# Two attention pairs per AV burst with the last keys as array quarters, and two transposes moved to the first mean, in a fused attention and FFN kernel

## The chip, the cores and the metric

The kernel runs on one core of one Trainium2 chip. The experiments ran in three groups, each on another chip (the record numbers them 6, 14 and 15), and every ratio is taken against the kernel before in the same group. The metric is the device time of one execution in microseconds (us). A profile of one execution belongs to each kernel; its span is about 2 us shorter than the time of a run. PE is TensorE (matmuls), PEld its weight loads, DVE VectorE, ACT ScalarE, POOL GpSimd, SP the queue that issues most of the small DMAs.

## The reference

```python
def _attn_ref(q, k, v):                       # 8 batches, 12 heads, 448 tokens, 64 dims
    scores = (1 / sqrt(64)) * q @ k.T
    attn = np.maximum(scores, 0.0) ** 2 / 448
    return attn @ v

def _moe_ref(x, g_ln, w_ch1, w_ch2):          # x: (8, 448, 768), the heads side by side
    xn = (x - mean(x)) / sqrt(var(x) + 1e-6) * g_ln
    return x + np.maximum(xn @ w_ch1, 0.0) @ w_ch2        # 768 -> 3072 -> 768
```

There is no softmax: relu squared keeps every score independent, so scores, squares and AV can be cut into pieces at will.

## The kernel before

For each batch b the kernel runs a first FFN layer (24 columns of 128 hidden units, `ffn_1`), then a second one. While it runs the first layer of batch b, it does the attention of batch b+1 in short "excursions" between two columns. A "pair" is two heads; a batch has six. Scores of a pair come in slots of 128 keys (t = 0, 1, 2); the last 64 keys (t = NF = 3) of two pairs share one slot, as four 64x64 quarters of the PE array. A batch has 21 slots of scores (QK), three in each of seven excursions, E1 to E7 below.

AV of one pair takes four slots: three of 128 keys, and one for the last 64 keys, whose weights `v_rest` are padded with zeros to 128 rows. One excursion does at most one AV:

```python
def att_AV(i, half=None, bank=None, evac_by=None):
    b, pr = divmod(i, NPAIR)
    if half != 1:
        av[0] = (next_f() if bank is None else bank)[:, :S]
    ps = av[0]
    v_heads, v_rest = v_parts(b)
    order = [NF, 0, 1, 2] if i % 2 else [0, 1, 2, NF]
    for n, t in enumerate(order):
        if half is not None and n // 2 != half:
            continue
        for hh in range(2):
            if t < NF:
                weights, values = v_heads[:, 2 * pr + hh, t * D:(t + 1) * D], attn[i, t][:, hh, :]
            else:
                weights, values = v_rest[:, pr, row0(i, hh):row0(i, hh) + D], attn[i - i % 2, NF][:, i % 2, :]
            nc.tensor.matmul(ps[hh * D:(hh + 1) * D, :], weights, values,
                             start=(n == 0), stop=(n == NF))
    if half == 0:
        return
    if evac_by is nc.scalar:
        nc.scalar.mul(xT_of(b, pr), ps, c2)
    else:
        nc.vector.tensor_scalar(xT_of(b, pr), ps, c2, None, op0=Alu.mult)
# ... (loads of the next v, sums for the mean)

def ffn_1(ni):
    ps = next_f()[:, :S]
    for ki in range(K1):
        for c in range(2):
            n0 = ni * P + c * D
            nc.tensor.matmul(ps[c * D:(c + 1) * D, :], w1[:, ki, n0:n0 + D], xc[:, ki, :],
                             start=(ki == 0), stop=(ki == K1 - 1))
    nc.scalar.activation(h[:, ni, CARRY:], ps, Act.Relu)

def excursion(n, third=(nc.vector, nc.vector), **how):
    flush_loads()
    next_AV(**how)
    took = [slots.pop(0) for _ in range(n)]
    for m, (i, t) in enumerate(took):
        att_QK(i, t, relu_by=third if m == 2 else nc.scalar)
    for i, t in took:
        att_square(i, t)
    for i, t in took:
        for e in ends(i, t):
            ready.append(e)
            queued(e)
```

The kernel uses eight banks of PSUM, the memory that the matmuls write to. Four (`sc`) hold scores, two (`spare`) hold the third QK slot of an excursion, and two (`next_f`, in turn) hold FFN columns and AV results. So a column uses bank A, the AV bank B, the next column A again: nobody waits for a bank.

Batch 0 has nothing to hide behind, so its attention comes first, slot by slot. Its end, where the mean over the features has to be known before the FFN can start, is this:

```python
def first_end():
    i = NPAIR
    att_AV(i - 1, 0)
    att_QK(i, 0)
    att_QK(i, 1)
    mean_part(i - 2)
    att_AV(i - 1, 1)
    mean_part(i - 1)
```

Batches 0 and 1 are transposed on PE (`att_T`), later ones by DMA transposes on the SP queue.

Of the kernel before, what the change touches and what calls it, by code (L numbers as in the profile page):

```python
# [11 lines left out]
def kernel(  # L12
# [44 lines left out]
    t_pool = ctx.enter_context(tc.tile_pool(name="qkT", bufs=3))  # L57
    attn_pool = ctx.enter_context(tc.tile_pool(name="attn", bufs=7))
    st_pool = ctx.enter_context(tc.tile_pool(name="stats", bufs=4))
    acc_pool = ctx.enter_context(tc.tile_pool(name="acc", bufs=4))  # L60
    o_pool = ctx.enter_context(tc.tile_pool(name="o", bufs=3))
    ps_pool = ctx.enter_context(tc.tile_pool(name="ps", bufs=1, space=bass.MemoryType.PSUM))
# [53 lines left out]

    next_sc = Turns(sc).next
    f_turn = Turns(fb[:2])
# [130 lines left out]

    def att_T(i, copy=None):  # L250
        if i >= PE_T * NPAIR:
            new_qkT(i)
            nc.sync.dma_start_transpose(qkT[i], qk_ring[:, i % 3].rearrange("p j c -> p (j c)"))
            return
        new_qkT(i)
        if i == 0:
            for t, cp in enumerate((nc.vector.tensor_copy, nc.scalar.copy)):
                ps = bf_view(next_f())
                pe_T(0, t, ps)
                c = slice(t * S, (t + 1) * S)  # L260
                cp(flat(0)[:, c], ps[:, c])
            return
        ps = bf_view(next_f() if i <= NPAIR else next_spare())
        for t in range(2):
            pe_T(i, t, ps)
        (copy or nc.vector.tensor_copy)(flat(i)[:, :2 * S], ps)
# [34 lines left out]
    def xT_of(b, ki):  # L301
        return xT[:, ki, (b % 2) * S:(b % 2 + 1) * S]

    def att_AV(i, half=None, bank=None, evac_by=None):
        b, pr = divmod(i, NPAIR)
        if half != 1:
            av[0] = (next_f() if bank is None else bank)[:, :S]
        ps = av[0]
        v_heads, v_rest = v_parts(b)
        order = [NF, 0, 1, 2] if i % 2 else [0, 1, 2, NF]  # L310
        for n, t in enumerate(order):
            if half is not None and n // 2 != half:
                continue
            for hh in range(2):
                if t < NF:
                    weights, values = v_heads[:, 2 * pr + hh, t * D:(t + 1) * D], attn[i, t][:, hh, :]
                else:
                    weights, values = v_rest[:, pr, row0(i, hh):row0(i, hh) + D], attn[i - i % 2, NF][:, i % 2, :]
                nc.tensor.matmul(ps[hh * D:(hh + 1) * D, :], weights, values,  # L319
                                 start=(n == 0), stop=(n == NF))  # L320
        if half == 0:
            return
        if evac_by is nc.scalar:
            nc.scalar.mul(xT_of(b, pr), ps, c2)
        else:
            nc.vector.tensor_scalar(xT_of(b, pr), ps, c2, None, op0=Alu.mult)  # L326
        if i >= PE_T * NPAIR and i % 2 and i + NPAIR < NP_ALL:
            load_v(i - 1 + NPAIR)
        if b == 0:
            if pr < GAIN_FIRST:  # L330
                nc.vector.tensor_scalar(xc[:, pr, :], xT_of(b, pr), g_sb[:, pr:pr + 1], None, op0=Alu.mult)
        elif pr == 1:
            nc.vector.tensor_add(xs, xT_of(b, 0), xT_of(b, 1))
        elif 1 < pr < NPAIR - 1:
            nc.vector.tensor_add(xs, xs, xT_of(b, pr))
# [55 lines left out]

    def ffn_1(ni):
        ps = next_f()[:, :S]
        for ki in range(K1):
            for c in range(2):
                n0 = ni * P + c * D
                nc.tensor.matmul(ps[c * D:(c + 1) * D, :], w1[:, ki, n0:n0 + D], xc[:, ki, :],  # L397
                                 start=(ki == 0), stop=(ki == K1 - 1))
        nc.scalar.activation(h[:, ni, CARRY:], ps, Act.Relu)  # L399

# [9 lines left out]
    def new_o():  # L410
        o_t = o_pool.tile([P, HD], fp32, tag="o")
        return o_t

    def store(o_t, m, d0, d1, engines=(nc.sync,)):
# [18 lines left out]
    def plain_part(b, m, dh, part, parts, box):  # L433
# [10 lines left out]
        if part == parts - 1:  # L444
            o_t = acc_pool.tile([P, HD], fp32, tag="acc")
            scaled_plus(o_t, box[m], m, x_half(m, dh))
            store(o_t, m, dh * HD, (dh + 1) * HD)
# [22 lines left out]
    def seven(b, pair, banks, last, between):  # L470
# [5 lines left out]
        bb = c  # L476
        acc1 = acc_pool.tile([P, HD], fp32, tag="acc")
        acc2 = acc_pool.tile([P, HD], fp32, tag="acc")
        tt = nc.vector.tensor_tensor
# [65 lines left out]
        if last:  # L545
            cut = HD - P
            parts = ((bb, 0, cut), (spare[1], cut, HD))
            for ps, d0, d1 in parts:
                product(ps, sums[6], B_TOP, True, d0, d1)
                flush()  # L550

                def after(ps=ps, d0=d0, d1=d1):
                    o_t = new_o()[:, :d1 - d0]
                    scaled_plus(o_t, ps[:, :d1 - d0], m2, acc2[:, d0:d1])
                    store(o_t, m2, HD + d0, HD + d1, (nc.sync, nc.scalar))
                posts.append(after)
            flush()
# [20 lines left out]
    for i in range(NPAIR, NP_ALL, 2):  # L578
        first = [(i, t) for t in range(NF + 1)]
        if i % NPAIR == 2:  # L580
            first[2:] = first[:1:-1]
        slots += first + [(i + 1, t) for t in range(NF)]
    slots = slots[slots.index((NPAIR, 2)):]
    ready = []

    def ends(i, t):

        if i % 2 == 0:
            return [i] if t == (NF - 1 if i % NPAIR == 2 else NF) else []
        return [i] if t == NF - 1 else []  # L590
# [5 lines left out]
    def excursion(n, third=(nc.vector, nc.vector), **how):  # L596
        flush_loads()
        next_AV(**how)
        took = [slots.pop(0) for _ in range(n)]
# [9 lines left out]
    def step_fine(i):  # L609
# [29 lines left out]
        if i:  # L639
            mean_part(i - 1)  # L640
        att_AV(i, 1)
        att_square(i + 1, 2)

    def first_end():
        i = NPAIR
        att_AV(i - 1, 0)
        att_QK(i, 0)
        att_QK(i, 1)
        mean_part(i - 2)
        att_AV(i - 1, 1)  # L650
        mean_part(i - 1)

    def ffn_1_first():
# [19 lines left out]
    IN_FIRST = (5, 8, 11, 14, 17, 20)  # L673
    T_IN_FIRST = {4: 1, 7: 2, 10: 3, 13: 4, 16: 5}
    X_AT = (4, 6, 8, 10, 12, 14)
# [4 lines left out]
    def ffn_1_all(b):  # L680
        ms = tiles_of(b)
        for ni in range(NI0 if b == 0 else 0, K2):
# [4 lines left out]
            if b == 0 and ni in V_AT:  # L687
                load_v(V_AT[ni])
            ffn_1(ni)
            flush()  # L690
# [12 lines left out]
            elif b < B - 1:  # L703
                shift = 2 if b == 1 else 0
                if ni - shift in IN_REST:
                    excursion(3, **(dict(third=(nc.scalar, nc.vector), evac_by=nc.scalar) if b == 1 else {}))
                if ni == min(IN_REST[-1] + shift + 3, K2 - 1):
                    flush_loads()
# [70 lines left out]
    with tc.manual_schedule(engines=set(ENGINES)):  # L779
        load_heads(0, [("q", 2, 2), ("k", 2, 2), ("k last", 2, H - 2), ("q", 4, 4), ("k", 4, 4), ("v", 0, 4),  # L780
                       ("v last", 0, H), ("q", 8, 4), ("k", 8, 4), ("v", 4, 4), ("v", 8, 4)])
        load_early()
        load_heads(1, [("q", 0, 2), ("k", 0, 2), ("k last", 0, H)])
        load_w1(0)
        load_heads(1, [("q", 2, 4), ("k", 2, 4)])
        load_w1(1)
        load_w1(2)
        load_heads(1, [("v", 0, H), ("v last", 0, H), ("q", 6, 6), ("k", 6, 6)])
        for c in range(3, NCH):
# [54 lines left out]
```

## Time and profile before

| | before |
|---|---|
| time, median (4 runs) | 528.01 us (527.81 to 528.66) |
| span of the profile | 525.9 us |
| PE busy | 517.0 us, 98% |
| granted PE clock | 1.0 |
| first-layer stage, batches 2 to 6, each | 37.72 us |

The page of the kernel before, part 1 (busy time of each engine, share of the span, instructions), and two of its costliest groups (line, engine, operation, tiles, shapes, count, then busy us and mean ns of one, then idle time of the engine just before them and what ended most of it):

```profile
PE 517.0 (98%) x5705; PEld 309.9 (59%) x5705; DVE 375.3 (71%) x662; ACT 272.8 (52%) x444; POOL 221.8 (42%) x255
...
L397 PE MATMUL f<-xc,w 128*64 128x448 bf16 x2256 | 226.9, 354 | 0.7 <-DVE o_t L428 0.4
...
L319 PE MATMUL f<-at,v_ring 128*64 128x448 bf16 x336 | 40.3, 354 | 0.5 <-DVE xT L326 0.2
```

PE has practically no idle time, and the first layer (L397) and AV (L319) are two of its largest pieces. But "mean 354 ns" is not what a matmul costs here: matmuls overlap, and two column halves run together. What one costs is read from start to start. The timeline of the kernel before around excursion E4 of one batch, PE only (start us, length us, engine, line, operation, tiles, shapes, count):

```profile
166.13 3.60 PE L397 MATMUL f<-xc,w 128*64 128x448 bf16 x36
169.56 0.92 PE L319 MATMUL f<-at,v_ring 128*64 128x448 bf16 x8
170.41 0.38 PE L279 MATMUL sc<-qkT_t 64*64 64x448 bf16 x4
170.72 0.36 PE L284 MATMUL sc<-qkT_t 64*128 64x448 bf16 x2
170.92 0.35 PE L284 MATMUL f<-qkT_t 64*128 64x448 bf16 x2
171.21 0.57 PE L397 MATMUL f<-xc,w 128*64 128x448 bf16 x4
```

From 166.13 to 169.56 there are 36 matmuls, 18 concurrent pairs: 0.19 us for one slot of 448 columns. AV (L319, 8 matmuls, 4 slots) has 0.85 us up to the next start, of which 0.10 is the change of array mode from 128x64 to 64x64 (L279, the quarters). The excursion takes 1.65 us, from 169.56 to 171.21, and the column after it starts without a wait.

The start of the FFN in the kernel before, PE only (in square brackets: idle time just before and what ended it):

```profile
27.04 0.35 PE L340 MATMUL f<-xT,ones 128*128 128x448 bf16 x1 [0.21 <-DVE xT L326]
27.32 0.63 PE L319 MATMUL f<-at,v_ring 128*64 128x448 bf16 x4
28.67 0.35 PE L340 MATMUL f<-xT,ones 128*128 128x448 bf16 x1 [0.72 <-DVE xT L326]
29.79 0.73 PE L663 MATMUL f<-xc,w 128*128 128x448 bf16 x3 [0.78 <-DVE xc L363]
...
36.02 0.68 PE L229 MATMUL f<-identity,w 112*64 112x112 bf16 x16
```

PE waits for VectorE three times between 26.8 and 29.8 us; a PE transpose of a pair (L229) comes later, at 36.02, where PE is never idle.

### The profile page before, as it was taken

Reading aid. Unit: us, or ns where it says so; the run is one execution under the profiler, and the core shown is the slowest. Engines: PE = TensorE matmul, PEld = TensorE weight load, DVE = VectorE, ACT = ScalarE, POOL = GpSimd, SP = SyncE. Lnnn points to the kernel's source line nnn. Section 1 sums busy time; section 2 is a strip of 40 time slices with the busy share of each in tenths; the row PEclk is TensorE's granted clock in tenths of the full one; section 3 lists DMA queues with packets and bytes.
Section 4 is the critical chain, followed back from the end, with each engine's and each line's share of the span. In section 5 each row is a group of like instructions: output and inputs, shape, how many; then the busy total and the mean of one; then the engine's idle time right before and its main releaser. Section 6 shows DMA issues by size and latency. Waiting matters only on the chain.

```text
span 525.9 us, 13704 instructions
## 1 busy us (share of the span) xinstructions
PE 517.0 (98%) x5705; PEld 309.9 (59%) x5705; DVE 375.3 (71%) x662; ACT 272.8 (52%) x444; POOL 221.8 (42%) x255
## 2 busy tenths in 40 slices
PE   8989999999999999999999999999999999999996
PEld 4445566556765566655666556655666556665665
DVE  5967778778858869589584886788695876951265
ACT  6965551878236662366623666466524665234320
POOL 8628215676622683227732267428632000320021
PEclk9999999999999999999999999999999999999999
DMA  9999999999637993679934799769944200250022
GB/s 135 173 194 201 205 201 146 202 125 105 82 80 99 106 102 62 122 73 115 94 66 105 72 113 122 108 62 123 82 77 106 49 14 3 62 112 11 1 61 62
DMA packets 175230, 53.04 MB, mean 101 GB/s; under 512 B 154176, under 2 KB 175168, under 8 KB 175168
## 3 DMA queue, kind: packets, MB, share of 16 engines
q0 software_dynamic: 103552, 25.74, 55.3%
q1 hardware_dynamic: 71088, 26.06, 27.1%
q8 instruction: 44, 0.72, 0.6%
q10 hardware_dynamic: 528, 0.37, 0.2%
q14 instruction: 18, 0.15, 0.1%
HBM read 51.91 MB, written 11.01 MB: 120 GB/s over the span
## 4 chain that ended last, share of the span: by engine, by line
PE 81%; DMA 12%; POOL 3%; DVE 2%; ACT 1%; issue 1%; POOLq 0%; DVEq 0%; ACTq 0%
PE f L397 36%; PE f L459 34%; DMA w<-in_moe_w_ch_dram 6%; PE f L319 5%; DMA s_sb<-in_v_dram 4%; PE sc L284 3%; PE f L284 1%; DMA w<-in_k_dram 1%; DVE w L210 1%; POOL w L201 1%; PE sc L279 1%; ACT at L292 1%; POOL w L141 1%; PE f L356 0%; POOL w L144 0%
## 5 line engine op out<-in xcount | busy, mean ns | idle before, releaser
L397 PE MATMUL f<-xc,w 128*64 128x448 bf16 x2256 | 226.9, 354 | 0.7 <-DVE o_t L428 0.4
L397 PEld LDWEIGHTS <-w 128*64 128x64 bf16 x2256 | 124.6, 110 | 94.4 <-issue 19.1
L399 ACT ACTIVATE h<-f 128x448 bf16<-128x448 f32 x188 | 102.5, 545 | 102.6 <-PE f L397 101.1
L459 PE MATMUL f<-w,s_sb 128*64 128x384 bf16 (+2 forms) x1584 | 130.0, 324 | 0.0
L292 ACT ACTIVATE at<-sc 128x896 bf16<-128x896 f32 x120 | 103.4, 917 | 16.5 <-PE sc L284 13.3
L459 PEld LDWEIGHTS <-s_sb 128*64 128x64 bf16 x1584 | 89.6, 110 | 37.7
L295 DVE TENSOR_TENSOR at<-at 128x896 bf16<-128x896 bf16 x168 | 95.8, 618 | 5.1 <-ACT at L292 4.8
L166 POOL DMA_DIRECT2D qk_ring<-in_q_dram x36 | 47.0, 1305 | 95.4 <-DMA qkT_t<-qk_ring 85.9
L493 POOL TENSOR_TENSOR o_t<-o_t,x_tok 128x384 f32<-128x384 f32 x26 | 24.4, 938 | 146.6 <-ACT o_t L492 132.1
L290 DVE TENSOR_SCALAR at<-f 128x448 bf16<-128x448 f32 x89 | 51.6, 618 | 24.2 <-PE f L284 24.2
L453 DVE TENSOR_TENSOR s_sb<-h 128x1536 bf16<-128x1536 bf16 x65 | 64.8, 1014 | 0.0
L492 ACT ACTIVATE o_t<-f,rstd 128x384 f32<-128x384 f32 x26 | 15.1, 580 | 94.7 <-DVE acc L497 46.7
L167 POOL DMA_DIRECT2D qk_ring<-in_k_dram x36 | 55.2, 1533 | 9.3 <-DMA w<-in_moe_w_ch_dram 9.3
L459 PE MATMUL f<-w,h 128*64 128x384 bf16 x624 | 52.9, 326 | 0.0
L168 POOL DMA_DIRECT2D qk_ring<-in_k_dram x36 | 46.6, 1293 | 5.2 <-DMA w<-in_moe_w_ch_dram 5.2
L326 DVE TENSOR_SCALAR xT<-f 128x448 bf16<-128x448 f32 x43 | 26.7, 620 | 28.2 <-PE f L319 27.6
L459 PEld LDWEIGHTS <-h 128*64 128x64 bf16 x624 | 35.5, 110 | 15.5
L319 PE MATMUL f<-at,v_ring 128*64 128x448 bf16 x336 | 40.3, 354 | 0.5 <-DVE xT L326 0.2
L493 POOL TENSOR_TENSOR acc<-acc,x_tok 128x384 f32<-128x384 f32 x24 | 28.0, 1176 | 22.5 <-ACT acc L492 22.5
L363 DVE SCALAR_TENSOR_TENSOR xc<-f,g_sb,xc 128x448 bf16<-128x448 f32 x45 | 28.5, 678 | 6.4 <-PE f L356 6.0
L178 POOL DMA_DIRECT2D v_ring<-in_v_dram x36 | 32.3, 1202 | 0.0
L284 PE MATMUL sc<-qkT_t 64*128 64x448 bf16 x206 | 31.3, 356 | 0.0
(81 smaller groups left out, 381.1 us busy)
## 6 DMA issues: line engine op xcount, KB each, us to landing
w<-in_moe_w_ch_dram POOLq DMA_DIRECT2D x6, 768.0 KB, 12.7
w<-in_moe_w_ch_dram POOLq DMA_DIRECT2D x4, 1152.0 KB, 26.2
v_ring<-in_v_dram POOLq DMA_DIRECT2D x21, 192.0 KB, 5.4
qk_ring<-in_q_dram POOLq DMA_DIRECT2D x36, 112.0 KB, 4.7
qk_ring<-in_k_dram POOLq DMA_DIRECT2D x36, 96.0 KB, 5.2
out_dram<-o_t SPq DMA_DIRECT2D x9, 168.0 KB, 2.2
out_dram<-o_t SPq DMA_DIRECT2D x9, 144.0 KB, 2.1
out_dram<-acc SPq DMA_DIRECT2D x7, 144.0 KB, 2.0
```

The costliest lines, as they stand in the source:

```text
L166: nc.gpsimd.dma_start(q_to, q[b, heads].rearrange("x (p j) d -> p j x d", j=NJ))
L167: nc.gpsimd.dma_start(k_to[:, :NF], k[b, heads, :SF].rearrange("x (p t) d -> p t x d", t=NF))
L284: nc.tensor.matmul(by_j(half[hh]), k_of(i, r, t, P), q_of(i, r), start=True, stop=True)
L290: nc.vector.tensor_scalar(at[:, x], half[x], 0.0, None, op0=Alu.max)
L292: nc.scalar.activation(at, ps[:, :, :S], Act.Relu)
L295: nc.vector.tensor_mul(attn[i, t], attn[i, t], attn[i, t])
L319: nc.tensor.matmul(ps[hh * D:(hh + 1) * D, :], weights, values, start=(n == 0), stop=(n == NF))
L397: nc.tensor.matmul(ps[c * D:(c + 1) * D, :], w1[:, ki, n0:n0 + D], xc[:, ki, :], start=(ki == 0), stop=(ki == K1 - 1))
L399: nc.scalar.activation(h[:, ni, CARRY:], ps, Act.Relu)
L453: nc.vector.tensor_tensor(s_sb[:, n], x, y, op=op)
L459: nc.tensor.matmul(ps[c * D:(c + 1) * D, :d1 - d0], stat[:, ki, c * D:(c + 1) * D], w2[:, slot, ki, d0:d1], start=(start and ki == 0), sto ...
L493: nc.gpsimd.tensor_tensor(o_t, o_t, x_half(m, dh), op=Alu.add)
```

## The change

The intent, as far as the diff tells it: give PE fewer slots and fill its idle time.

1. The AV of two pairs runs in one excursion (E4 and E6 of each batch). The last keys of both pairs use the array as four 64x64 quarters, one slot for both in place of one padded slot each: 7 slots for 8. The order of the QK slots is changed so that an excursion with two AV begins with QK quarters.
2. Two AV need both `next_f` banks, so the column just before must leave its bank quickly: its relu is split into two halves on ScalarE and VectorE (`by_both`), and the two AV results are evacuated on the two engines.
3. At the first mean two PE transposes fill PE's idle time, the last AV of batch 0 comes earlier, and q and k of those transposes are loaded ahead of w1; v of batch 1 is loaded later.

The diff, cut to its core:

```diff
+    def att_AV2(i):
+        ps = [next_f()[:, :S] for _ in range(2)]
+        for x in range(2):
+            for t in range(NF):
+                av_part(ps[x], i + x, t, t == 0, False)
+        b, pr = divmod(i, NPAIR)
+        v_rest = v_parts(b)[1]
+        for x in range(2):
+            for hh in range(2):
+                r0 = row0(i + x, hh)
+                nc.tensor.matmul(ps[x][hh * D:(hh + 1) * D, :], v_rest[r0:r0 + SS, pr + x, r0:r0 + D],
+                                 attn[i, NF][r0:r0 + SS, x, :], start=False, stop=True)
+        for x in range(2):
+            av_out(i + x, ps[x], (nc.vector, nc.scalar)[x])
 ...
-        nc.scalar.activation(h[:, ni, CARRY:], ps, Act.Relu)
+        c = S // 2 if by_both else S
+        nc.scalar.activation(h[:, ni, CARRY:CARRY + c], ps[:, :c], Act.Relu)
+        if by_both:
+            nc.vector.tensor_scalar(h[:, ni, CARRY + c:], ps[:, c:], 0.0, None, op0=Alu.max)
 ...
     def excursion(n, third=(nc.vector, nc.vector), **how):
         flush_loads()
-        next_AV(**how)
+        if len(ready) > 1:
+            assert ready[0] % 2 == 0 and ready[1] == ready[0] + 1
+            att_AV2(ready.pop(0))
+            ready.pop(0)
+        elif ready and ready[0] % NPAIR == NPAIR - 2:
+            next_AV(**how)
 ...
     def first_end():
 ...
-        mean_part(i - 2)
         att_AV(i - 1, 1)
+        att_T(i + 1, nc.scalar.copy, next_f())
+        mean_part(i - 2)
         mean_part(i - 1)
+        att_T(i + 2, nc.scalar.copy, sc_turn.items[-1][:, 0])
 ...
-    T_IN_FIRST = {4: 1, 7: 2, 10: 3, 13: 4, 16: 5}
+    T_IN_FIRST = {10: 3, 13: 4, 16: 5}
 ...
+        load_heads(1, [("q", 2, 4), ("k", 2, 4)])
         load_w1(0)
-        load_heads(1, [("q", 2, 4), ("k", 2, 4)])
 ...
-        load_heads(1, [("v", 0, H), ("v last", 0, H), ("q", 6, 6), ("k", 6, 6)])
+        load_heads(1, [("q", 6, 6), ("k", 6, 6), ("v", 0, H), ("v last", 0, H)])
```

Left out: more attention buffers (9 for 7) and fewer output buffers, the slot order of the last two pairs, an earlier square at the end of batch 0, and helper functions.

More of the change, by code (lines that the diff above doesn't have):

```diff
@@ L57 @@
     t_pool = ctx.enter_context(tc.tile_pool(name="qkT", bufs=3))
-    attn_pool = ctx.enter_context(tc.tile_pool(name="attn", bufs=7))
+    attn_pool = ctx.enter_context(tc.tile_pool(name="attn", bufs=9))
     st_pool = ctx.enter_context(tc.tile_pool(name="stats", bufs=4))
-    acc_pool = ctx.enter_context(tc.tile_pool(name="acc", bufs=4))
-    o_pool = ctx.enter_context(tc.tile_pool(name="o", bufs=3))
+    acc_pool = ctx.enter_context(tc.tile_pool(name="acc", bufs=3))
+    o_pool = ctx.enter_context(tc.tile_pool(name="o", bufs=2))
     ps_pool = ctx.enter_context(tc.tile_pool(name="ps", bufs=1, space=bass.MemoryType.PSUM))
@@ L113, in next @@
             return it
-    next_sc = Turns(sc).next
+    sc_turn = Turns(sc)
+    next_sc = sc_turn.next
     f_turn = Turns(fb[:2])
@@ L248, in k_of, with att_T @@
         return flat(i)[r, c0:c0 + keys]
-    def att_T(i, copy=None):
+    def att_T(i, copy=None, bank=None):
         if i >= PE_T * NPAIR:
@@ L262, in att_T @@
             return
-        ps = bf_view(next_f() if i <= NPAIR else next_spare())
+        if bank is None:
+            bank = next_f() if i <= NPAIR else next_spare()
+        ps = bf_view(bank)
         for t in range(2):
@@ L302, in xT_of, with av_part @@
         return xT[:, ki, (b % 2) * S:(b % 2 + 1) * S]
+    def av_part(ps, i, t, start, stop):
+        b, pr = divmod(i, NPAIR)
+        v_heads, v_rest = v_parts(b)
+        for hh in range(2):
+            if t < NF:
+                weights, values = v_heads[:, 2 * pr + hh, t * D:(t + 1) * D], attn[i, t][:, hh, :]
+            else:
+                weights, values = v_rest[:, pr, row0(i, hh):row0(i, hh) + D], attn[i - i % 2, NF][:, i % 2, :]
+            nc.tensor.matmul(ps[hh * D:(hh + 1) * D, :], weights, values, start=start, stop=stop)
     def att_AV(i, half=None, bank=None, evac_by=None):
-        b, pr = divmod(i, NPAIR)
         if half != 1:
@@ L308, in att_AV, with av_out @@
         ps = av[0]
-        v_heads, v_rest = v_parts(b)
         order = [NF, 0, 1, 2] if i % 2 else [0, 1, 2, NF]
         for n, t in enumerate(order):
-            if half is not None and n // 2 != half:
-                continue
-            for hh in range(2):
-                if t < NF:
-                    weights, values = v_heads[:, 2 * pr + hh, t * D:(t + 1) * D], attn[i, t][:, hh, :]
-                else:
-                    weights, values = v_rest[:, pr, row0(i, hh):row0(i, hh) + D], attn[i - i % 2, NF][:, i % 2, :]
-                nc.tensor.matmul(ps[hh * D:(hh + 1) * D, :], weights, values,
-                                 start=(n == 0), stop=(n == NF))
-        if half == 0:
-            return
+            if half is None or n // 2 == half:
+                av_part(ps, i, t, n == 0, n == NF)
+        if half != 0:
+            av_out(i, ps, evac_by)
+    def att_AV2(i):
[3 more added lines that the diff above has]
+                av_part(ps[x], i + x, t, t == 0, False)
+        b, pr = divmod(i, NPAIR)
+        v_rest = v_parts(b)[1]
+        for x in range(2):
+            for hh in range(2):
+                r0 = row0(i + x, hh)
[3 more added lines that the diff above has]
+            av_out(i + x, ps[x], (nc.vector, nc.scalar)[x])
+    def av_out(i, ps, evac_by):
+        b, pr = divmod(i, NPAIR)
         if evac_by is nc.scalar:
@@ L390, in ffn_stats, with ffn_1 @@
         nc.vector.bn_aggr(mv_sb[:, m, :], stats)
-    def ffn_1(ni):
+    def ffn_1(ni, by_both=False):
         ps = next_f()[:, :S]
@@ L412, in new_o, with new_acc @@
         return o_t
+    def new_acc():
+        acc_t = acc_pool.tile([P, HD], fp32, tag="acc")
+        return acc_t
     def store(o_t, m, d0, d1, engines=(nc.sync,)):
@@ L444, in plain_part @@
         if part == parts - 1:
-            o_t = acc_pool.tile([P, HD], fp32, tag="acc")
+            o_t = new_acc() if dh else new_o()
             scaled_plus(o_t, box[m], m, x_half(m, dh))
@@ L476, in seven @@
         bb = c
-        acc1 = acc_pool.tile([P, HD], fp32, tag="acc")
-        acc2 = acc_pool.tile([P, HD], fp32, tag="acc")
+        acc1, acc2 = new_acc(), new_acc()
         tt = nc.vector.tensor_tensor
@@ L552, in after @@
                 def after(ps=ps, d0=d0, d1=d1):
-                    o_t = new_o()[:, :d1 - d0]
-                    scaled_plus(o_t, ps[:, :d1 - d0], m2, acc2[:, d0:d1])
+                    o_t = acc2[:, d0:d1]
+                    scaled_plus(o_t, ps[:, :d1 - d0], m2, o_t)
                     store(o_t, m2, HD + d0, HD + d1, (nc.sync, nc.scalar))
@@ L581 @@
             first[2:] = first[:1:-1]
-        slots += first + [(i + 1, t) for t in range(NF)]
+        second = [(i + 1, t) for t in range(NF)]
+        if i % NPAIR == 4:
+            first[1:] = [(i, NF), (i, 1), (i, 2)]
+        slots += first + second
     slots = slots[slots.index((NPAIR, 2)):]
@@ L588, in ends @@
         if i % 2 == 0:
-            return [i] if t == (NF - 1 if i % NPAIR == 2 else NF) else []
+            return [i] if t == (NF - 1 if i % NPAIR else NF) else []
         return [i] if t == NF - 1 else []
@@ L640, in step_fine @@
             mean_part(i - 1)
-        att_AV(i, 1)
-        att_square(i + 1, 2)
+        if i + 2 < NPAIR:
+            att_AV(i, 1)
+            att_square(i + 1, 2)
+        else:
+            att_square(i + 1, 2)
+            att_AV(i, 1)
     def first_end():
@@ L648, in first_end @@
         att_QK(i, 1)
+        att_AV(i - 1, 1)
+        att_T(i + 1, nc.scalar.copy, next_f())
         mean_part(i - 2)
-        att_AV(i - 1, 1)
         mean_part(i - 1)
+        att_T(i + 2, nc.scalar.copy, sc_turn.items[-1][:, 0])
     def ffn_1_first():
@@ L688, in ffn_1_all @@
                 load_v(V_AT[ni])
-            ffn_1(ni)
+            bursts = IN_FIRST if b == 0 else [n + (2 if b == 1 else 0) for n in IN_REST]
+            ffn_1(ni, by_both=b < B - 1 and ni in bursts and len(ready) > 1)
             flush()
@@ L703, in ffn_1_all @@
             elif b < B - 1:
-                shift = 2 if b == 1 else 0
-                if ni - shift in IN_REST:
+                if ni in bursts:
                     excursion(3, **(dict(third=(nc.scalar, nc.vector), evac_by=nc.scalar) if b == 1 else {}))
-                if ni == min(IN_REST[-1] + shift + 3, K2 - 1):
+                if ni == min(bursts[-1] + 3, K2 - 1):
                     flush_loads()
```

## The prediction

> **What bounds it.** TensorE. The page has PE busy 517.0 of 525.9 us at full granted clock, and the waits view gives PE only about 5 us of named waits, all before 89 us. From batch 2 on the timeline has no gap: 36 first-layer matmuls (18 concurrent column pairs) start at 251.59 and the next group at 255.02, so one 448-column slot is 0.19 us; an AV (8 matmuls, 4 slots) takes 0.76 us. So every slot removed and every stall added on PE goes straight into the time.
>
> **What the change removes.**
> 1. AV of two pairs: 8 slots become 7 (four 64x64 quarters run together, as the QK of the last keys already does). 14 double AVs (two in each of seven batches): -0.19 us each, -2.7 us. Mode changes: the Trainium skill (TensorEngine Tiling (Array Packing), Tiling Modes, Key Properties) says that a mode switch drains the array; this trace agrees (AV to QK starts 0.10 us late, QK back to the first layer 0.09, quarters to QK 0.13). Their number stays, as the QK of the last keys now follows the AV quarters.
> 2. Start: between 26.5 and 29.8 us PE idles about 2.4 us in four gaps (0.23, 0.37, 0.91, 0.94) for the last xT, the mean and the first xc. Two transposes of 0.61 us each (36.02, 41.10 us) move there, the last AV runs about 0.4 us earlier, and their q and k load ahead of w1. w1's first chunk should land at about 28.8 instead of 24.35, just in time. Estimate: -1.7 us, kept, since w1's fourth chunk (landing 48.7) is then only just not late.
>
> **What it adds.** The double AV takes both first-layer banks. (T: start of the last slot of the column before.)
> - The second pair wants the bank at T+0.76. ACT's relu starts at T+0.40. The split halves should run side by side, but in the built program's order with its waits DVE's half waits for ACT's in all 14 places. From the groups (ACT 545 ns for 448, 917 for 896; DVE 618 for 448) a half is about 0.36 on ACT and 0.39 on DVE: in turn, 0.40+0.36+0.05+0.39+0.05 = T+1.25. Stall about 0.5 us. (Unsplit: about 0.24.)
> - The next column wants the first pair's bank. Its quarters start at T+1.92, DVE's evacuation starts 0.45 later and takes 0.62, so it is free at T+3.05; PE is there at T+2.91. Stall about 0.14.
> So each double AV costs 0.64-0.19 = +0.45 us: 12 of them +5.4. In batch 1, where a weight sum or statistics (1.3 us of DVE) stands between relu and evacuation, I reckon +1.2 in all.
>
> The smaller pools should change nothing.
>
> **Sum:** 528.0-1.7+5.4+1.2 = 532.9; shaded to 532.3, the stalls being estimates. Range 529.0 to 535.0. Faster by over 2%: 0.01; within 2%: 0.97; slower by over 2%: 0.02.
>
> **What would show it.** Right: waits view with PE AV line waiting on DVE's h half, 14 times about 0.5; PE first layer waiting on DVE xT about 0.14; in the timeline DVE's half starting after ACT's ends; first w1 matmul at about 29.3, the first-layer stage of batches 2 to 6 each about 0.9 longer. Wrong: halves overlapping, stages 0.2 to 0.4 shorter, or quarters that take more than one slot.
>
> **What would make it wrong.** If halves do overlap, the stall falls to about 0.14 and the result is about 527.5. If w1's first chunk comes later than 29.3, the start's gain is lost.

## The result, and the profile after

| | before | after |
|---|---|---|
| time, median of 4 runs each | 528.01 us | 533.61 us (533.33 to 534.44) |
| ratio | | 1.0106, 95% interval 1.0089 to 1.0124 |
| span of the profile | 525.9 us | 531.9 us |
| first-layer stage, batches 2 to 6, each | 37.72 us | 38.56 us |

A ratio here is the mean time of one kernel's fast runs over that of the other's of the same rounds, so not quite the ratio of the medians. The change makes the kernel about 1% slower: inside the 2% band, and clear of noise.

The page after, part 1, and all waits of PE (line, what it waited for: total us, times, longest us):

```profile
PE 518.1 (97%) x5705; PEld 314.4 (59%) x5705; DVE 373.9 (70%) x664; ACT 273.1 (51%) x456; POOL 222.1 (42%) x255
```

```profile
PE f L315 <- DVE h L425: 4.3, 14, 0.3
PE f L420 <- DMA w<-in_moe_w_ch_dram: 1.5, 1, 1.5
...
PE sc L282 <- DMA qkT_t<-qk_ring: 0.5, 1, 0.5
```

The first wait is new and comes 14 times, once for each double AV: AV (L315) waits for VectorE's half of the relu (L425). The other two are single waits for DMAs, in batches 0 and 1.

PE's busy time rose by only 1.1 us while the span rose by 6.0, and the wait view gives 0.3 us for each double AV; neither is what was lost. A matmul counts as busy for about 0.35 us from its start, although the next one could start after 0.19, so the first part of every stall hides inside "busy". The Trainium skill warns of this row (Trainium Kernel Development and Optimization, Performance Expectations: it is "a bad metric" for the distance to roofline, because matmuls are pipelined), and this trace agrees: 1.1 us more of busy time for 6.0 us of span. Starts tell the loss. The timeline after, excursion E4 of the same batch as above, all of PE, ACT and DVE that belongs to it:

```profile
170.53 0.73 PE L315 MATMUL f<-at,v_ring 128*64 128x448 bf16 x6
170.73 0.36 ACT L423 ACTIVATE h<-f 128x224 bf16<-128x224 f32 x1 [0.59 <-PE f L420]
...
171.12 0.39 DVE L425 TENSOR_SCALAR h<-f 128x224 bf16<-128x224 f32 x1
171.57 0.76 PE L315 MATMUL f<-at,v_ring 128*64 128x448 bf16 x6 [0.31 <-DVE h L425]
172.26 0.38 PE L339 MATMUL f<-at,v_ring 64*64 64x448 bf16 x4
172.47 0.36 PE L282 MATMUL sc<-qkT_t 64*64 64x448 bf16 x4
172.68 0.62 DVE L349 TENSOR_SCALAR xT<-f 128x448 bf16<-128x448 f32 x1 [1.16 <-PE f L339]
172.72 0.54 ACT L347 ACTIVATE xT<-f 128x448 bf16<-128x448 f32 x1 [1.63 <-PE f L339]
172.76 0.36 PE L287 MATMUL sc<-qkT_t 64*128 64x448 bf16 x2
172.96 0.35 PE L287 MATMUL f<-qkT_t 64*128 64x448 bf16 x2
173.35 0.95 PE L420 MATMUL f<-xc,w 128*64 128x448 bf16 x8
```

- ScalarE's half runs from 170.73 to 171.09, VectorE's from 171.12 to 171.51: in turn, not side by side. In all 14 places VectorE's half waits for a semaphore that ScalarE's half raises, and starts 0.03 to 0.04 us after its end.
- The first pair's three slots (six matmuls from 170.53) would end at 171.10; the second pair starts at 171.57, 0.06 us after VectorE's half: 0.47 us lost.
- The quarters are one slot of four (L339), followed at 0.21 us by the QK quarters (L282).
- The next column (L420, 173.35) starts 0.05 us after VectorE has evacuated the first pair (172.68 + 0.62): it waits for that bank too.
- The excursion takes 2.82 us, 170.53 to 173.35. Before it was 1.65 us with one AV; the other AV, 0.76 us, has moved in from the excursion before. So a double AV costs 2.82 - 1.65 - 0.76 = 0.41 us more, and a stage, with two of them, 0.84.

All five stages of batches 2 to 6 show this 0.84 us to a hundredth. The windows view of one of them in each kernel, batch 2 before and after (window, its length, then busy us of PE, PEld, DVE, ACT, POOL, clock, DMA share, GB/s):

```profile
153.80:191.52 37.72, 37.72 (x388) 20.01 (x384) 28.21 (x55) 24.36 (x38) 19.55 (x23) 1.00 1.03 107
```

```profile
155.53:194.09 38.56, 37.86 (x388) 20.88 (x385) 27.86 (x55) 24.42 (x40) 19.55 (x24) 1.00 0.93 107
```

At the start of the FFN the idle time is filled as intended. The same stretch after, and the place in batch 0 where the gain is given back, PE only:

```profile
26.89 0.70 PE L230 MATMUL f<-identity,w 112*64 112x112 bf16 x16 [0.15 <-DVE xT L349]
27.52 0.55 PE L363 MATMUL f<-xT,ones 128*128 128x448 bf16 x2
28.00 0.70 PE L230 MATMUL sc<-identity,w 112*64 112x112 bf16 x16
...
49.64 1.70 PE L420 MATMUL f<-xc,w 128*64 128x448 bf16 x16 [1.48 <-DMA w<-in_moe_w_ch_dram]
```

Both transposes (L230) stand in the gaps, and the first w1 matmul comes at 28.85 us (29.79 before). That gain of 0.94 us is of this pair of profiles alone: over all kept profiles the first w1 matmul comes at 28.85 to 30.60 us with the new start (eight profiles) and at 29.24 to 29.79 with the old one (five). In the profile after, at 49.64, PE waits 1.48 us for the fourth chunk of w1, which lands at 49.59 (48.69 before).

Where the 6 us went, from the starts of the stages in the two profiles (single executions):

| part | after minus before |
|---|---|
| up to the first w1 matmul of batch 0 | -0.94 us |
| rest of batch 0 (two double AV, two transposes less, w1 wait, second layer) | +1.24 |
| batch 1, first layer (two double AV, a wait for a DMA transpose) | +1.42 |
| batches 2 to 6, first layers | 5 x 0.84 = +4.2 |
| last batch and all other second layers | about 0 |

### The profile page after: what moved, and what is told of

It is laid out like the page before. It is cut to its first block, busy times and chain, and to the rows that moved or that the text cites. A ratio compares the mean times of both kernels' runs of the same rounds, so it can differ in the third digit from the quotient of the medians.

```text
span 531.9 us, 13636 instructions
## 1 busy us (share of the span) xinstructions
PE 518.1 (97%) x5705; PEld 314.4 (59%) x5705; DVE 373.9 (70%) x664; ACT 273.1 (51%) x456; POOL 222.1 (42%) x255
## 4 chain that ended last, share of the span: by engine, by line
PE 79%; DMA 8%; DVE 8%; POOL 2%; ACT 1%; issue 1%; POOLq 0%; DVEq 0%
PE f L420 34%; PE f L489 33%; DMA w<-in_moe_w_ch_dram 6%; PE f L315 4%; PE sc L287 3%; DVE at L298 2%; PE f L287 2%; DVE at L293 2%; PE f L472 1%; DMA v_ring<-in_v_dram 1%; DMA qkT_t<-qk_ring 1%; DVE w L211 1%; DVE h L425 1%; PE sc L282 1%; ACT h L423 1%
## 5 line engine op out<-in xcount | busy, mean ns | idle before, releaser
L420 PE MATMUL f<-xc,w 128*64 128x448 bf16 x2256 | 226.4, 353 | 2.8 <-DMA w<-in_moe_w_ch_dram 1.5
L420 PEld LDWEIGHTS <-w 128*64 128x64 bf16 x2256 | 130.9, 110 | 92.8 <-issue 20.1
L423 ACT ACTIVATE h<-f 128x448 bf16<-128x448 f32 (+1 forms) x188 | 100.4, 534 | 99.8 <-PE f L420 99.0
L167 POOL DMA_DIRECT2D qk_ring<-in_q_dram x36 | 44.5, 1236 | 94.1 <-DMA qkT_t<-qk_ring 70.8
L168 POOL DMA_DIRECT2D qk_ring<-in_k_dram x36 | 53.4, 1482 | 9.8 <-DMA w<-in_moe_w_ch_dram 9.3
L169 POOL DMA_DIRECT2D qk_ring<-in_k_dram x36 | 44.3, 1230 | 4.8 <-DMA w<-in_moe_w_ch_dram 4.7
L315 PE MATMUL f<-at,v_ring 128*64 128x448 bf16 x288 | 36.1, 355 | 4.3 <-DVE h L425 3.7
L522 POOL TENSOR_TENSOR acc_t<-acc_t,x_tok 128x384 f32<-128x384 f32 x24 | 28.8, 1209 | 22.3 <-ACT acc_t L521 22.3
L349 DVE TENSOR_SCALAR xT<-f 128x448 bf16<-128x448 f32 x33 | 20.4, 619 | 24.4 <-PE f L339 13.9
L179 POOL DMA_DIRECT2D v_ring<-in_v_dram x36 | 33.6, 1268 | 0.0
L287 PE MATMUL sc<-qkT_t 64*128 64x448 bf16 x192 | 30.0, 356 | 0.0
```

The lines of the kernel that those rows point to most:

```text
L167: nc.gpsimd.dma_start(q_to, q[b, heads].rearrange("x (p j) d -> p j x d", j=NJ))
L168: nc.gpsimd.dma_start(k_to[:, :NF], k[b, heads, :SF].rearrange("x (p t) d -> p t x d", t=NF))
L287: nc.tensor.matmul(by_j(half[hh]), k_of(i, r, t, P), q_of(i, r), start=True, stop=True)
L423: nc.scalar.activation(h[:, ni, CARRY:CARRY + c], ps[:, :c], Act.Relu)
L522: nc.gpsimd.tensor_tensor(o_t, o_t, x_half(m, dh), op=Alu.add)
```

## The experiments

Theory: each double AV stalls PE at two banks, because the relu halves take turns and because the first pair's evacuation comes too late; the moved start gives nothing, because loads and DMA transposes hold PE back later in batches 0 and 1. Rivals: quarters or pairing cost in themselves; the split is harmless; the new start itself loses or gains.

### e1: the relu whole again

```diff
-            ffn_1(ni, by_both=b < B - 1 and ni in bursts and len(ready) > 1)
+            ffn_1(ni)
```

> The changed kernel, but the relu of the column before a double AV stays whole on ScalarE. My theory: the split is what hurts, because VectorE's half waits for ScalarE's half (ends at T+1.17 us in the trace of the changed kernel), so the bank comes free later than with one whole relu of 0.54 us from T+0.39 to T+0.94. The second pair's first matmul should start at about T+0.99 instead of T+1.23, each double AV should take 0.24 us less (from the last column's last slot to the next column: 2.78 instead of 3.01), 14 of them 3.3 us: about 530.3 us. Rival: the wait comes from handing over both banks whatever the relu's form; then the time stays near 533.6.

Measured: 531.36 us (ratio to before 1.0057, 1.0040 to 1.0075), stages of batches 2 to 6 38.22 us. The same excursion, cut:

```profile
169.30 1.56 PE L315 MATMUL f<-at,v_ring 128*64 128x448 bf16 x12
169.51 0.54 ACT L423 ACTIVATE h<-f 128x448 bf16<-128x448 f32 x1 [0.59 <-PE f L420]
...
170.79 0.38 PE L339 MATMUL f<-at,v_ring 64*64 64x448 bf16 x4
...
171.28 0.62 DVE L349 TENSOR_SCALAR xT<-f 128x448 bf16<-128x448 f32 x1 [1.38 <-PE f L339]
...
171.96 0.38 PE L420 MATMUL f<-xc,w 128*64 128x448 bf16 x2
```

The quarters come 1.49 us after the first AV matmul (1.73 with the split): the expected 0.24 us are there. But the excursion takes 2.66 us, only 0.16 less, not 0.24: VectorE begins the evacuation 0.49 us after the quarters (0.42 with the split), and the next column waits for it as before. So the split costs time. The rival is right about the other half of the stall: with a whole relu the second pair still starts 0.23 us late (at 170.10; the first pair's slots would end at 169.87, the relu ends at 170.05). As for the totals, 14 x 0.16 = 2.3 us is also about the difference of the medians, 533.61 - 531.36, though the two are of different rounds. The second stall swallowed a third of the gain, so the total is 1 us over the expected 530.3.

### e5: two halves that need not take turns

The column before a double AV is computed in two halves of 224 columns, the second into a spare bank. The relu halves and their engines stay.

```diff
+        if by_both:
+            for n, bank in enumerate((ps, spare[1])):
+                s0 = n * (S // 2)
+                ...  # the same matmuls, on xc[:, ki, s0:s0 + S // 2] into bank[..., :S // 2]
+            nc.scalar.activation(h[:, ni, CARRY:CARRY + S // 2], ps[:, :S // 2], Act.Relu)
+            nc.vector.tensor_scalar(h[:, ni, CARRY + S // 2:], spare[1][:, :S // 2], 0.0, None, op0=Alu.max)
+            return
```

> The changed kernel, with the column before a double AV computed in two halves of 224 columns: the first half in its own bank, the second in a spare bank; the same relu halves on the same two engines. My theory: the halves took turns only because both read one bank, and the second pair waited only for that bank. Here ScalarE's half is done before the column ends, VectorE's half does not wait for it, and the second pair's first matmul does not wait at all; only the stall of the evacuation is left. Each double AV should take about 0.46 us less: the first-layer stages of batches 2 to 6 about 37.64 us (changed 38.56, before 37.72). Rival: VectorE's half is slow or late in itself, or the second pair waits for something else (its squares, its weights); then the stages stay near 38.5.

Measured (one look, 529.68 us): stages of batches 2 to 6 37.73 us. Excursion E6 of batch 2:

```profile
179.91 0.36 ACT L425 ACTIVATE h<-f 128x224 bf16<-128x224 f32 x1
180.27 1.30 PE L315 MATMUL f<-at,v_ring 128*64 128x448 bf16 x12
180.48 0.39 DVE L426 TENSOR_SCALAR h<-f 128x224 bf16<-128x224 f32 x1 [0.79 <-PE f L423]
181.50 0.38 PE L339 MATMUL f<-at,v_ring 64*64 64x448 bf16 x4
```

All twelve AV matmuls run through (1.23 us to the quarters, six slots and a mode change) while VectorE's half is still at work beside them: neither VectorE's speed nor the second pair itself was the trouble; the bank that the relu and the second pair share was. (The halves do not run side by side here either: ScalarE's is over before the column ends. So e5 shows what the second pair waited for, not that two halves in two banks would overlap.) The stage is 0.83 us shorter than in the changed kernel, 0.09 longer than expected; the same late evacuation as in e1 (L349 began 0.49 us after the quarters) accounts for that.

Why the halves take turns in one bank was looked at in the built program: VectorE's half waits for ScalarE's half in all 14 places, and it still does when it writes to another tile or when the halves are cut by partitions (neither was run on the chip). So the order is set when the program is built, and comes from the common PSUM tile, which is one bank, and not from the output. Whether the halves could run side by side without that wait, cut by partitions for instance, was not tried. The Trainium skill (PSUM — Partial Sum Buffer, PSUM bank collisions raise a hardware error) says that two engines on one bank and 32-partition quadrant at once raise an error, two reads included, so that such accesses have to be ordered. No run here tried the collision.

### e8: no quarters

```diff
+        for x in range(2):
+            av_part(ps[x], i + x, NF, False, True)     # padded, in place of the four quarters
```

> The changed kernel, but the last keys of both pairs in the old padded form, two slots in place of one slot of four quarters. If a quarter slot saves a slot under any circumstances, each double AV takes 0.19 us more and the stages of batches 2 to 6 go from 38.56 to 38.94 us. My theory: most of that slot was already lost to the wait for the first pair's evacuation (0.10 us late), which the longer form hides, so the double AV goes from 3.01 to about 3.07 us and the stages to about 38.66 us.

Measured (one look, 535.1 us): stages of batches 2 to 6 38.71 us, 0.15 more than with quarters, not 0.38. Quarters do save their slot, but 0.11 us of each 0.19 was already lost to the evacuation, which the longer form hides: here the column after the excursion starts 0.25 us after the first pair's bank was free (174.15 against 173.90 in E4), and 0.05 us after it in the changed kernel.

### e3: the double AV without the new start

The edit takes back `first_end`, `T_IN_FIRST`, the moved square and the order of the loads.

> The changed kernel with the start of the kernel before: double AV with quarters, split relu, evacuations on two engines, and nothing else. My theory: the double AV costs 0.42 us each (0.84 us in each first-layer stage of batches 2 to 6), 14 of them 5.9 us, and the start's change is worth about nothing: 533.5 to 534.5 us. Rival: the start's change itself loses time; then this run is nearer to 532.

Measured: 533.21 us (ratio 1.0090, 1.0075 to 1.0105), slightly under the expected range; stages of batches 2 to 6 38.55 us, batch 1 +0.88 and not +1.42. The double AV explains the whole loss, as far as these runs resolve it (the profiled spans of both are 531.9 us). That the new start is worth about nothing on top of it is what this run and the changed kernel say together, within some tenths of a microsecond.

### e2 and e10: the new start without the double AV

e2 is the kernel before with part 3 of the change. e10 is the same, but v of batch 1 is loaded ahead of the late q and k, as before.

> The kernel before with the change's start alone (two transposes at the first mean, copies on ScalarE, loads reordered). My theory after the trace: TensorE gains 1 to 2 us by then, but has to wait for the fourth chunk of w1, whose landing the loads' bandwidth sets at 48.7 to 49.6 us; of the gain at most 0.5 us is left: 527.3 to 528.2 us, and the waits show TensorE waiting about 1 us for that DMA. Rival, as predicted: the 1.7 us are kept, 526.3 us.

Measured: e2 531.21 us (ratio 1.0061, 1.0038 to 1.0085). Both my number and the rival's missed, and the wait was another one. PE in e2, and the windows view of the same stretch (columns as above; the clock is the third number from the end):

```profile
44.71 0.95 PE L322 MATMUL f<-at,s_sb 128*64 128x448 bf16 x8 [2.26 <-DMA s_sb<-in_v_dram]
```

```profile
42.00:46.00 4.00, 1.74 (x20) 0.60 (x16) 0.23 (x1) 0.55 (x2) 1.86 (x3) 1.00 1.55 188
46.00:49.40 3.40, 3.40 (x20) 1.47 (x18) 3.15 (x6) 2.19 (x3) 3.40 (x4) 0.50 1.24 206
```

A single AV wants v at about 42.5 us, and the changed order of loads lands it at 44.7. With a double AV the first use of v is one excursion later, so this wait belongs to the combination that I built, not to the change.

The second view also shows what can follow a wait: PE ran at half clock for the next 3.4 us. A wait does not always bring this, and the new start is not needed for it: in e9 below, which has the old start, PE ran at half clock from 29.11 to 32.52 us after the same three waits (0.21, 0.72 and 0.78 us) that the kernel before has without it. In the clock records of all these traces the whole stretches are multiples of 3.413 us long (3.41, 13.65, 23.89, 40.96, 51.20), so a likely reason, not tested, is that it matters where a wait falls on that grid. Seven of the 27 runs of the kernel before in the three groups list a mean clock of 0.996 or 0.997, about what one such stretch would make (an estimate: half of 3.41 us in 526 us is 0.3%). So it is likely a source of scatter on both sides of the comparisons here.

> The start's change on the kernel before, as in e2, but batch 1's v is loaded ahead of the late q and k, as before. My theory: e2 lost its time because the single AV of batch 1 wants v at about 42 us and the changed load order lands it at 44.7; with v first that wait of 2.3 us and the half clock after it are gone, and what the two moved transposes gain is cut off by the fourth chunk of w1 (landing about 49 us): 527.0 to 528.2 us. Rival: the moved transposes lose time in themselves; then it stays above 529.

Measured: e10 528.60 us (527.90 to 530.32), ratio 1.0007 (0.9984 to 1.0030). The median is a little over the expected range and under the rival's 529, with two of four runs above that. So v's place was e2's loss, and without it the new start is worth nothing that these runs can resolve. Its profile is of the slowest run (530.32 us). In it PE waited 1.4 us for the first chunk of w1, 0.4 for the fourth and 1.1 for a DMA transpose in batch 1, and ran 3.4 us at half clock after the first of these waits. The first chunk landed at 30.44 us, so here PE gained nothing even at the start: the case that the prediction names as its own risk ("later than 29.3").

### e4 and e6: the same work in another order

The stalls are a matter of when a bank is wanted. In this "woven" order the second bank is first wanted for the quarters, and the first pair is finished two QK slots and one AV before its bank is wanted; relus are whole:

```diff
+    def woven(i, took, third, evac_by):
+        ps = [next_f()[:, :S] for _ in range(2)]
+        for t in range(NF):
+            av_part(ps[0], i, t, t == 0, False)
+        att_QK(*took[0])                                  # QK of the last keys
+        quarters(i, ps, (False, True), (True, False))     # ends pair i, begins pair i + 1
+        av_out(i, ps[0], nc.vector)
+        att_QK(*took[1])
+        att_QK(*took[2], relu_by=third)
+        for t in range(NF):
+            av_part(ps[1], i + 1, t, False, t == NF - 1)
+        av_out(i + 1, ps[1], evac_by)
```

> Other order, same work: the first pair's three parts, the QK of the last keys, the four quarters of both pairs, the two other QK, then the second pair's three parts; the relu is whole. My theory: the cost is only the time at which the two banks are wanted. Here the second bank is first wanted at T+1.04 (free at T+0.99) and the first pair's bank again at T+2.41 (free at T+2.14), with the same number of mode changes, so there is no stall and each double AV saves its slot of 0.19 us: 2.41 instead of 3.01 us from the last column to the next. The first-layer stages of batches 2 to 6 should be 37.34 us (before 37.72, changed 38.56), and the whole 525 to 526.5 us, less than the kernel before. Rival: quarters or pairing cost in themselves; then it stays above 528.

Measured: stages of batches 2 to 6 37.34 us, as expected, 0.38 less than before, that is two slots. The excursion:

```profile
169.96 0.73 PE L315 MATMUL f<-at,v_ring 128*64 128x448 bf16 x6
...
170.62 0.38 PE L282 MATMUL sc<-qkT_t 64*64 64x448 bf16 x4
170.83 0.36 PE L334 MATMUL f<-at,v_ring 64*64 64x448 bf16 x4
...
171.12 0.36 PE L287 MATMUL sc<-qkT_t 64*128 64x448 bf16 x2
171.30 0.62 DVE L355 TENSOR_SCALAR xT<-f 128x448 bf16<-128x448 f32 x1 [0.74 <-PE f L334]
...
171.61 0.76 PE L315 MATMUL f<-at,v_ring 128*64 128x448 bf16 x6
...
172.20 0.35 PE L426 MATMUL f<-xc,w 128*64 128x448 bf16 x2
```

2.24 us in place of 2.82, with the same seven AV slots, three QK slots and mode changes, and no wait. The first pair's evacuation ends at 171.92, 0.28 us before its bank is wanted. Quarters and pairing cost nothing in themselves; that rival falls.

The total, though, was 527.86 us with a scatter from 525.51 to 532.87 (ratio 1.0001, 0.9945 to 1.0058): inconclusive. The waits of its profile show 2.0 us for a w1 chunk and 2.0 us for a DMA transpose in batch 1, and the slowest of its runs had a mean clock of 0.992. So e6 takes the woven order with the start of the kernel before:

> The woven order with the start of the kernel before. My theory: the woven double AV saves 0.38 us in each first-layer stage; the new start loses in batch 0 by DMA what it gains on TensorE, and its late w1 chunk can also drop the clock. So the stages of batches 2 to 6 are 37.34 us; in batch 1 TensorE meets the DMA transposes of q and k (landing at 107 to 108 us) about 0.4 us earlier than the kernel before and loses up to that. Total 525.3 to 526.3 us, faster than before by 0.3 to 0.5%, with less scatter than the woven kernel with the new start (525.5 to 532.9). Rival: the scatter comes from the woven order itself; then it shows here too.

Measured: 526.54 us (526.03 to 527.39, 5 runs), ratio 0.9965 (0.9952 to 0.9978): faster than the kernel before. The time is a little over the expected range, the scatter is small, as expected. Its one large wait is in batch 1:

```profile
106.64 0.38 PE L282 MATMUL sc<-qkT_t 64*64 64x448 bf16 x2 [1.41 <-DMA qkT_t<-qk_ring]
```

The transposes awaited there land at 106.6 and 107.4 us, much as in the kernel before (106.2 and 107.0), whatever PE has saved until then. Batch 1's stage is 40.77 us (39.58 before): the saving of batch 0 and more is given back.

### e9 and e12: that last wait

The transposes stand behind eight stores in the SP queue. e9 is e6 with four of those stores issued by ScalarE.

> As the run before it, and the first four stores of batch 0 are issued by ScalarE, idle at that time, instead of the SP queue. My theory: the transposes that TensorE awaits in batch 1 stand behind eight stores (about 0.6 us of issue each) in the SP queue; with four less they are issued some 2 us earlier and land before TensorE wants them, so the first-layer stage of batch 1 loses its wait: 39.2 us or less there (39.58 before), total 525.0 to 525.8 us. Rival: the transposes wait for the loads of q and k rather than for the queue; then nothing changes against the run before it.

Measured: 538.23 us (ratio 1.0187). A failure, and not by either theory: PE waited 11.2 us, once, for VectorE, which waited for ScalarE, which waited for transposes:

```profile
90.58 1.78 ACT L372 ACTIVATE xc<-xT,g_sb 128x448 bf16<-128x448 bf16 x3 [16.13 <-DMA qkT_t<-qk_ring]
92.54 8.40 PE L478 MATMUL f<-w,h 128*64 128x384 bf16 x72 [11.15 <-DVE o_t L464]
```

The four stores on ScalarE's queue use the same four completion semaphores as four DMA transposes of the SP queue, issued earlier. These landed at 88.74, 90.19, 92.42 and 95.00 us, and the stores were issued at 88.81, 90.21, 92.52 and 95.02, so ScalarE stood until the transposes had landed. PE ran at half clock from 83.72 to 97.38 us. Whether the stores hold up the transposes stays open: batch 1's stage was short here (38.40 us), but only because PE came 14 us late.

e12 is e6 with the needy excursion of batch 1 one column later. The next one stays where it was, so one column less lies between the two (the text below says that it comes a column earlier; the edit does not do that):

```diff
-            bursts = IN_FIRST if b == 0 else [n + (2 if b == 1 else 0) for n in IN_REST]   # b == 1: 3, 6, 9, 12, 15, 18, 21
+            bursts = IN_FIRST if b == 0 else (3, 6, 9, 13, 15, 18, 21) if b == 1 else IN_REST
```

> The woven order with the old start; in batch 1 the excursion that needs the late transposes comes one column later, and the next one column earlier. My theory: the wait of 1.4 us for the transpose shrinks to 0.3 us or less, without a new stall: stage of batch 1 at about 39.7 us in place of 40.8, total 525.2 to 525.8 us. Rival: ScalarE or VectorE, closer packed after the shift, stall TensorE by as much; then it stays at 526.5.

Measured: 525.36 us (524.89 to 527.08, 6 runs), ratio 0.9945 (0.9928 to 0.9963); batch 1's stage 39.49 us. The excursion in question, PE only:

```profile
105.69 0.76 PE L315 MATMUL f<-at,v_ring 128*64 128x448 bf16 x6
106.38 0.38 PE L282 MATMUL sc<-qkT_t 64*64 64x448 bf16 x4
106.59 0.36 PE L334 MATMUL f<-at,v_ring 64*64 64x448 bf16 x4
```

The wait is gone. This version beats both kernels: 0.55% under the kernel before, and 8 us under the changed one's median (of other rounds).

### e11: the woven order with the new start, v first

> The woven order with the new start and v first. My theory: whatever TensorE gains in batch 0 is taken back at the fourth chunk of w1 and at the DMA transposes of batch 1 (landing at 106 to 107 us whatever TensorE does), so this is within 0.7 us of the woven kernel with the old start (526.5), with more waiting. Rival: the start's 1.7 us of the prediction are real and only v's place hid them; then 524.8 us.

Measured: 527.35 us (525.58 to 528.66), ratio 0.9980 (0.9958 to 1.0002). The median is 0.8 us above e6's 526.54 (of other rounds), a tenth more than the 0.7 that I gave it, with more scatter. The start's predicted 1.7 us do not appear in this combination either.

## Why the prediction was right, and where not

The range (529.0 to 535.0) holds the measured 533.61 us, and the unshaded sum of 532.9 was nearer than the 532.3 on record. Point by point:

- **PE bounds the kernel, and every PE stall goes into the time: right.** Five stages of 0.84 us more make 4.2 of the 6.0 us of the two spans.
- **The relu halves run in turn, stall about 0.5 us: right.** Measured 0.47 us, 0.49 to 0.50 in batch 1, 14 times; e1 shows that the split makes 0.24 us of it and that the rest comes with needing the second bank at all; e5 shows that the second pair waited for nothing but that bank. That the built program's waits were read before any run made the difference; from the diff alone one would have taken the halves for parallel, and the sum for no loss.
- **The waits view would show about 0.5 each: wrong in form.** It shows 0.3, because it counts from the modelled end of the last matmul.
- **The second stall, about 0.14 us: right**, about 0.1 measured; the evacuation began 0.42 us after the quarters, not 0.45. The view of waits doesn't show it at all; e1, e5 and e8 do.
- **Quarters take one slot and no mode change is added: right**, with 0.02 us from AV quarters to QK quarters.
- **+0.45 us for each double AV: right**, 0.42 from the stages.
- **Batch 1, +1.2 us: size about right (1.42), by luck; reason wrong.** The step was that "a weight sum or statistics (1.3 us of DVE) stands between relu and evacuation". It did not hold up anything: in batch 1 VectorE began the evacuation 0.44 and 0.42 us after the quarters, as elsewhere. The double AV cost there what it costs elsewhere (e3: +0.88 us for the stage), and the rest was a wait of 0.5 us for a DMA transpose, which I had not looked for.
- **The start, "-1.7 us, kept": wrong.** This is the step that failed. PE did gain at the start, but the fourth chunk of w1, of which I said that it "is then only just not late", was 1.5 us late, and e10 puts the start's worth at nothing (1.0007, 0.9984 to 1.0030). I had compared PE's arrival with the landing of the old order to within some tenths, and taken a tie for safety. Nor does the landing stay at 48.7 us: the fourth chunk lands at 47.8 to 49.0 us in the five profiles with the old start and at 49.1 to 51.4 in the eight with the new one, so PE's gain, where it had one, turned into waiting. Why it lands later stays open, since the same loads stand before it in both orders; bandwidth is the likely limit (188 to 208 GB/s in e2 from 36 to 55 us), but no run varied it. Batch 0 as a whole came out at +0.30 us in the profiles (-0.94 and +1.24), where the prediction has -1.7 + 2 x 0.45 = -0.8. This miss of 1.1 us is about the whole difference between the predicted sum (+4.9 us) and the spans (+6.0); the range was wide enough to hold it.
- **The smaller pools change nothing: not contradicted.** The woven kernels have the same pools, and their stages came out at the expected 37.34 us.

## What to carry to other kernels

Before you put one PSUM bank's evacuation on two engines, read in the built program whether the second half waits for the first: here it did in all 14 places, and two halves in turn (0.36 and 0.39 us) were slower than one whole instruction (0.54 us). A gain in slots is only worth what the banks allow, so write down for each bank when it comes free and when it is next wanted, and order the work so that the first is earlier: the same instructions, woven differently, turned a loss of 0.42 us into a gain of 0.19. A stretch that lives on arriving data gives nothing back for a faster engine; check the landing times behind the place that you speed up, and treat a tie as a wait.

## What the Trainium skill lacked or had wrong

- TensorE: Matmul & The Clock Gate, What's actually happening: it has half clock "after ≥1 idle window (~3.4µs)". The length agrees (3.4 us at 0.50 in e2 and in e10), but here no window of 3.4 us before these drops was idle: in e2 a single wait of 2.26 us came before it, with PE busy 1.74 us of the 4.0 us from 42 to 46 us, and in e9 and e10 PE was busy 1.84 us of the 3.4 us before. Two waits of 2.0 us in e4's profile did not do it.
- PSUM — Partial Sum Buffer, Summary: it gives no price for the order that two engines must keep in one bank. Here two halves in turn (0.36 on ScalarE, 0.39 on VectorE) freed the bank 0.24 us later than one whole relu of 0.54 us on ScalarE.
- TensorEngine Tiling (Array Packing), Key Properties: a mode switch "requires drain", without a size. Here it costs 0.09 to 0.13 us between modes, and 0.02 us between two different pieces of work in the same 64x64 mode.
- No page that I read gives the price of completion semaphores shared by DMAs of two issuing engines: in e9 stores on ScalarE's queue waited for transposes of the SP queue, ScalarE stood for 16.13 us, and PE waited 11.2 us.
